# Halves of a matrix check spread among its rows, and one raw place more kept for the FFN's weights

## The chip, the core and the metric

The kernel runs on one core of one Trainium2 chip. The metric is the device time of one execution in microseconds (us). The kernel before took 197.28 us, the median of 3 runs (195.94 to 198.41).

## What is computed

All arrays are fp32, x is 2048 tokens by 576. The reference mixes by two Fourier matrices, adds the residual, picks the one token with the highest router score, and sends that token alone through a SwiGLU FFN of 4608 columns:

```python
a = einsum("bsd,ed->bse", layernorm(x), dft_hid_re); b = einsum("bsd,ed->bse", layernorm(x), dft_hid_im)
h = x + einsum("ts,bse->bte", dft_seq_re, a) - einsum("ts,bse->bte", dft_seq_im, b)
n = layernorm(h);  r = n @ w_r;  i = argmax(r)
y = (silu(n[i] @ w_gate) * (n[i] @ w_up)) @ w_down * sigmoid(r[i])
out = h + n;  out[i] += y
```

## The kernel before

The sequence matrices (`ct`) are cosines and sines, so a quarter of them, folded, is enough for the product, provided that what is left out mirrors what is used. The kernel does not take that on trust: it loads the mirrored parts too and compares them. Should a comparison fail, a general path that stands behind a branch computes everything again. So two streams run side by side: the products (PE) and the comparisons (VectorE subtracts or adds two tiles into a buffer Q of two slots, and ScalarE squares and sums a slot, `L405`, 2944 wide for a full slot).

**Two groups.** The row blocks of `ct` are worked off as group zero, `[1..5]`, and group one, `[6, 7, 0, 8]`. Each block has a cosine (0) and a sine part (1). The parts that are multiplied are kept in 14 places of D: D0 (5 places), D1 (5) and D2 (4); D0 serves group zero's cosines and later group one's sines. What is only compared goes through 8 raw places R0 to R7 (R0 to R2 are 1152 wide, R3 to R7 896), or through a D place that has come free.

**Comparisons.** A *row comparison* (`c_check`) compares one block with its mirror, which GpSimd gathers (`load_c`, 0.46 MB, 128 x 896), and, if the block has a partner (16 minus its number), the partner's block, which SyncE loads (0.59 MB, 128 x 1152), and the partner's mirror. These are the VectorE instructions of `L418` and `L420`, two of 896 and one of 1152 elements a row; `L418` is the form that also sums, used while a spill flag is open or for the last, the *gate* comparison, (8, 1). A *half comparison* (`c_half`, `off_h`) compares the two halves of blocks in D: group zero's three are on VectorE (`L449`, blocks 0 and 1, 2 and 3, and 4 of the group, cosine and sine), group one's on GpSimd (`L447`), behind the gate comparison. `w_check` and `wc_check` compare the hidden matrix W in the same way; `w_first` and `wc_first` load it.

**Products.** For each group five sequence products (`seq_step`, PE, `L641`, into PSUM tiles ps_0 to ps_4, the last 64 wide in two parts), each drained by ScalarE (a copy, `os`, `L655`) and VectorE (into Z, `L659`) in `keep_step`. PSUM has two pairs of banks for them: a product can start when Z of the last but one is out of its pair. The right-hand operand is XF, the folded and normalised x. Then the hidden products (`hid_step`, PE, `L686`, py), residual sums on VectorE (`L695`), sums of squares on ScalarE (`L718`), and router dots on VectorE (`L699`).

**The order.** The program is written as a plan: `add` names an engine, a duration in us, and what an operation needs; `Plan.order` is a list scheduler that puts the operations of all engines into the order in which they are issued, by the longest way to the end. The loads of one queue stay in the order in which the program asks for them. `ring` hands out the first free place of a list; a place is put back on that list when the program has asked for the row's comparison. So the order of the calls `c_half`, `c_check`, `w_first` decides which place each load gets, and after which comparison its engine may issue it.

**FFN weights.** They come as 1.18 MB loads (`load_ffn`, `L1330`, SyncE) into 16 spots that reuse XF, D, R, W, Z and Q. The order of loads is gate, up and down for four columns at a time. A load waits for the last reader of its spot, and everything behind it in SyncE's queue waits too. `LEFT` names raw places that, from a given row of group one on, the row comparisons do not take any more (the set `shut` in `ring`), so that the FFN weights find them free. The chosen token's products with gate and up are on VectorE (`L1347`, `L1354`) and GpSimd (`L1358`), the sums on ScalarE (`L1363`), the down product on PE (`L1384`).

Of the kernel before, what the change touches and what calls it, by code (L numbers as in the profile page):

```python
# [37 lines left out]
GROUPS = [[1, 2, 3, 4, 5], [6, 7, 0, 8]]  # L38
# [5 lines left out]
HALVES = [[(0, 2), (2, 2), (4, 1)], [(0, 2), (2, 2)]]  # L44
# [17 lines left out]
LATE = 6  # L62


LEFT = {(7, 0): (0, 1)}

# [7 lines left out]
class Plan:  # L76
# [6 lines left out]
    def add(self, eng, dur, fn, *deps, tail=0.0, push=0.0, holds=False, moves=False):  # L83
        flat = []
        for d in deps:
            flat += d if isinstance(d, list) else [d]
        n = {"eng": eng, "dur": dur, "fn": fn, "deps": [d for d in flat if d], "tail": tail, "push": push}
        n["holds"], n["moves"] = holds, moves
        n["i"] = len(self.ops)
        self.ops.append(n)  # L90
        return n
# [72 lines left out]
def kernel(  # L164
# [272 lines left out]
    def half_on_pool(g, c, i):  # L437
        return g == 1
# [343 lines left out]
    def then(f, *args):  # L782
        return lambda: f(*args)
# [41 lines left out]
    for a, b in X_RUNS:  # L825
# [4 lines left out]
        m = [add("ACT", 0.95, then(measure, k), f, push=push) for k, f in zip(ks, r)]  # L830
# [28 lines left out]
    for k in FOLDED:  # L859
        dg, use, at = [], [], []  # L860
        for sl in slots_of(k):
            n = next(places)
            UF[sl] = LATER[n]
            at.append(PLACE[n])
            if k in PAIRS:
                u, w = dgs.take()
# [42 lines left out]
    def c_load(j, i, mirror):  # L909
        CU[j, i, mirror] = ring("POOL" if mirror else "SP", load_c, 0.46 if mirror else 0.59, j, i, mirror)  # L910

    def c_first(g, i, cs=None):

        for c, j in enumerate(GROUPS[g]):
            if cs is not None and c not in cs:
                continue
            u = D_TAG[g, i], c
            if u in free:
                free.remove(u)
            w, users[u] = users[u], []  # L920
            LAST["SP"], d = load("SP", then(load_c, None, j, i, False), 0.59, w, LAST["SP"])
            CU[j, i, False] = u, d

    def c_half(g, c, m):
        u, w = qs.take()
        cus = [[CU[j, i, False] for j in GROUPS[g][c : c + m]] for i in range(2)]
        n = [
            add(
                *(("POOL", 0.3 + 1.31 * m) if half_on_pool(g, c, i) else ("DVE", 0.16 + 0.62 * m)),
                then(off_h, g, c, m, i, u), [d for _, d in cus[i]], w, PASSED if half_on_pool(g, c, i) else None,  # L930
                holds=not half_on_pool(g, c, i),
            )
            for i in range(2)
        ]
        for i in range(2):
            for b, _ in cus[i]:
                users[b].append(n[i])
        if (g, c + m) == (1, len(GROUPS[1])):
            HELD.append((u, 9 * m * P, n))
            return  # L940
        squares(u, 9 * m * P, n)
# [5 lines left out]
    def squares(u, w, n, ps=P, behind=None):  # L947
        SQUARES.append(add("ACT", 0.3 + w / 1200, then(square, u, w, ps), n, behind))
        qs.users[u].append(SQUARES[-1])

    def c_check(j, i):

        u, w = qs.take()
        u0, d0 = CU[j, i, False]
        c_load(j, i, True)
        u1, d1 = CU[j, i, True]
        n = [add("DVE", 1.08, then(off_s, j, i, u, 0), d0, d1, w, holds=True)]
        if (j, i) == GATE:
            PASSED.append(add("POOL", 0.1, lambda: pool.tensor_copy(gate[:, 1:2], gate[:, 0:1]), n))
        users[u0] += n  # L960
        users[u1] += n
        free.append(u1)
        if j in PAIRS:
            m = NK - j
            c_load(m, i, False)
            c_load(m, i, True)
            (u2, d2), (u3, d3) = CU[m, i, False], CU[m, i, True]
            n.append(add("DVE", 1.08, then(off_s, m, i, u, 1), d2, d3, w, holds=True))
            users[u3].append(n[1])
            n.append(add("DVE", 1.36, then(off_t, j, i, u), d0, d2, w, holds=True))  # L970
            users[u0].append(n[2])
            users[u2] += n[1:]
            free.extend([u3, u2])
        if u0[0] == "D1":
            free.append(u0)
        squares(u, QW if j in PAIRS else 7 * P, n)
# [3 lines left out]
    def w_first():  # L980
        for n in range(3):
            LAST["SP"], d = load(
                "SP", then(load_w, None, n), (0.59, 0.59, 0.005)[n], LAST["SP"], users["W" + "ABC"[n]]
            )
            WL.append(d)

    def wc_first():
        LAST["POOL"], d = load("POOL", then(load_w, None, 5), 0.295, LAST["POOL"])
        WC.append(d)

    def w_check():
        for n in range(2):
            u, d = ring("POOL", load_w, 0.59, n + 3)
            q, w = qs.take()
            o = add("DVE", 2.2, then(off_w, n, q), WL[n], d, w, holds=True)
            users[u].append(o)
            squares(q, 3 * D, o)
            WS.append(o)
            free.append(u)

    def wc_check():
        q, w = qs.take()
        WS.append(add("DVE", 2.6, then(off_wc, q), WL[2], WC, w))
        squares(q, D + 289, WS[-1])
# [91 lines left out]
        for b in [b for b in free if type(b) is tuple and b[0] == tag]:  # L1096
            free.remove(b)

    for c, m in HALVES[0]:
        c_half(0, c, m)  # L1100
    for n, j in enumerate(GROUPS[0]):
        if n == 3:
            w_first()
        if n == 3:
            wc_first()
        c_check(j, 0)
    for n in (0, 1, 4, 2, 3):
        seq_step(0, n)
        keep_step(0, n)
# [8 lines left out]
    no_more("D2")  # L1118
    free += [("D0", n) for n in range(N_D["D0"])]
    rows, first = iter(GROUPS[0]), iter(range(len(GROUPS[1])))  # L1120
    for step in "sffsffwcsss":
        if step == "s":
            c_check(next(rows), 1)
        elif step == "f":
            c_first(1, 0, (next(first),))
        elif step == "c":
            wc_check()
        else:
            w_check()
    no_more("D0")  # L1130
    c_first(1, 1)
    for i in range(2):
        for j in GROUPS[1]:
            shut.update(LEFT.get((j, i), ()))
            c_check(j, i)
# [103 lines left out]
    step = add("DVE", 0.25, T["steps"][0], SCORES)  # L1239
    most = add("PE", 0.4, T["steps"][1], step)  # L1240
    step = add("DVE", 0.45, T["steps"][2], step)
    step = add("PE", 0.4, T["steps"][3], step, most)
    qx = add("DVE", 0.4, from_result, SCORES)
    rows = add("DVE", 0.55, T["steps"][4], most)
    slot = add("DVE", 1.1, token, step, rows)
    step = add("DVE", 1.0, where, slot, qx)
    step = add("ACT", 2.0, row_of_token, step, slot, RESULTS)
    squares(*HELD[0], behind=step)
    near = add("POOL", 1.0, other_rows, slot, push=50.0)
    step = add("PE", 1.2, to_all, step)  # L1250
# [33 lines left out]
    for b in range(NJ // TW):  # L1284
        j = TW * b
# [202 lines left out]
    with tc.If(T["mv"], preferred_fallthrough_block=False):  # L1488
        with ExitStack() as gen:
# [33 lines left out]
            with ExitStack() as hs:  # L1523
# [9 lines left out]
                with tc.For_i(0, NK, 1) as k:  # L1533
                    dve.tensor_copy(xr, row_of(GX, k))
                    norm(xn, xr, "x")
                    for a in range(5):
                        w = min(P, D - a * P)
# [4 lines left out]
                    for c in range(4):  # L1542
                        pa = zbank(f"gpa{c}")
                        for a in range(5):
                            w = min(P, D - a * P)
# [115 lines left out]
```

## Time and profile before

| | |
|---|---|
| median of 3 runs (197.28 to compare with) | 197.28 us |
| range of the runs | 195.94 to 198.41 us |
| the profiled execution's own time | 197.32 us |
| its span on the core | 195.3 us |
| PE, weight load, VectorE, ScalarE, GpSimd busy | 67%, 46%, 84%, 72%, 61% of the span |
| moved by DMA | 77.74 MB, mean 398 GB/s |

All rows that are shown come from the one profiled execution, whose clock starts with the span; 2.0 us of its time lie around the span. Engines: PE is TensorE's matmul, DVE VectorE, ACT ScalarE, POOL GpSimd, SP SyncE; a q behind the name is the sequencer that issues DMAs. `L420` is line 420 of the kernel before; tiles have their names without numbers. In a timeline a row gives the start, the time from the first instruction's start to the last one's end, engine, line, operation, the tile written and the tiles read, their shape, and how many instructions stand in it; in square brackets how long the engine was idle before, and what ended it.

### The profile page before, as it was taken

What the parts mean: (1) busy time and instruction counts of PE and PEld (TensorE: products, weight loads), DVE (VectorE), ACT (ScalarE), POOL (GpSimd) and SP (SyncE); (2) the same over time, 40 slices, a digit from 0 to 9 for tenths busy, and PEclk for the clock granted to TensorE, in tenths of its full rate; (3) what the DMA queues carried; (4) which work ended last, traced back from release to release, by engine and by line L of the source; (5) the groups of instructions that cost most, each with busy time, mean ns of one, the idle gap of its engine ahead of it and who ended that gap; (6) DMA issues with size and microseconds to landing.
All of it is one profiled execution on the core that took longest, in us unless ns stands there. A gap on an engine that the chain in (4) does not pass through costs nothing.

```text
span 195.3 us, 2824 instructions
## 1 busy us (share of the span) xinstructions
PE 130.8 (67%) x758; PEld 89.9 (46%) x758; DVE 163.7 (84%) x430; ACT 140.4 (72%) x260; POOL 119.3 (61%) x152
## 2 busy tenths in 40 slices
PE   0007999999999999999699989800241425073960
PEld 0005667765767788677576767500121212030340
DVE  2399999999899999997799999999739999979620
ACT  3298854782898697499289979697679898986600
POOL 6588888761515874076170006968639999999500
PEclk9999999999999999999999999985555555555599
DMA  5999999999999999999999999999999999999992
GB/s 182 414 413 411 412 411 406 411 403 396 408 410 411 413 404 406 408 413 411 407 403 392 422 428 393 422 410 368 425 426 425 416 433 425 421 419 416 411 425 92
DMA packets 14483, 77.74 MB, mean 398 GB/s; under 512 B 1911, under 2 KB 1915, under 8 KB 11134
## 3 DMA queue, kind: packets, MB, share of 16 engines
q1 hardware_dynamic: 10340, 56.34, 71.5%
q0 software_dynamic: 4112, 21.17, 26.8%
q8 instruction: 7, 0.11, 0.2%
q14 instruction: 14, 0.11, 0.2%
q10 hardware_dynamic: 10, 0.00, 0.0%
HBM read 72.78 MB, written 6.49 MB: 406 GB/s over the span
## 4 chain that ended last, share of the span: by engine, by line
DVE 31%; POOL 15%; issue 15%; DMA 11%; PE 5%; ACT 2%; ACTq 0%; SPq 0%; POOLq 0%; DVEq 0%
DVE Q L420 11%; POOL D L1358 8%; DMA R<-in_ct_dram 7%; DVE junk L699 6%; DMA D<-in_wt_dram,iw 4%; DVE X L695 4%; PE pd L1384 3%; DVE Z L659 2%; POOL R L1358 2%; DVE Q L418 2%; PE pk L1392 2%; POOL R L333 1%; POOL W L1358 1%; ACT Q L405 1%; POOL Q L1358 1%
## 5 line engine op out<-in xcount | busy, mean ns | idle before, releaser
L405 ACT ACTIVATE Q<-Q 128x2944 bf16<-128x2944 bf16 (+5 forms) x26 | 54.7, 2104 | 12.7 <-DVE Q L420 7.6
L686 PE MATMUL py<-W,Z 128*128 128x289 f32 x180 | 45.3, 409 | 1.0 <-DVE X L695 1.0
L641 PE MATMUL ps<-D,XF 128*128 128x320 f32 (+3 forms) x216 | 44.9, 407 | 1.6 <-DVE Z L659 1.6
L333 POOL DMA_INDIRECT R<-in_ct_dram,ic x22 | 24.7, 1121 | 27.3 <-DVE Q L420 15.9
L686 PEld LDWEIGHTS py<-W,Z 128*128 128x128 f32 x180 | 33.7, 189 | 12.3 <-PE py L686 1.8
L641 PEld LDWEIGHTS ps<-D,XF 128*128 128x128 f32 (+1 forms) x216 | 32.2, 172 | 13.8 <-issue 3.2
L1358 POOL TENSOR_TENSOR D<-D,Z 128x1152 f32<-128x1152 f32 x7 | 18.3, 2642 | 0.0
L574 ACT ACTIVATE junk<-X,XT 128x576 bf16<-128x576 f32 x16 | 12.3, 771 | 7.5 <-DVE W L535 6.3
L718 ACT ACTIVATE junk<-X,TD 128x576 bf16<-128x576 f32 x16 | 12.3, 768 | 5.4 <-DVE X L695 5.3
L420 DVE TENSOR_TENSOR Q<-D 128x896 bf16<-128x896 f32 (+1 forms) x13 | 15.0, 1186 | 1.0 <-ACT Q L405 1.0
L418 DVE SCALAR_TENSOR_TENSOR Q<-R,D 128x896 bf16<-128x896 f32 (+1 forms) x11 | 13.4, 1216 | 2.9 <-DMA R<-in_ct_dram 2.7
L420 DVE TENSOR_TENSOR Q<-R,D 128x896 bf16<-128x896 f32 (+1 forms) x13 | 15.0, 1163 | 0.0
L613 PE MATMUL fo<-W,diag 128*128 128x288 f32 (+1 forms) x8 | 4.2, 706 | 16.0 <-DVE diag L604 16.0
L333 POOL DMA_INDIRECT D<-in_ct_dram,ic x10 | 11.9, 1189 | 4.0 <-DVE Q L420 1.8
L699 DVE SCALAR_TENSOR_TENSOR junk<-X,wrz 128x576 bf16<-128x576 f32 x16 | 12.0, 752 | 0.4
L748 ACT ACTIVATE X<-X,BB,UP 128x576 f32<-128x576 f32 x14 | 10.9, 852 | 2.0 <-DVE BB L731 2.0
L695 DVE SCALAR_TENSOR_TENSOR X<-py,X 128x576 f32<-128x576 f32 x16 | 11.7, 753 | 0.0
L1384 PE MATMUL pd<-XF,H 128*1 128x144 f32 x80 | 5.1, 406 | 9.8 <-DVE H L1376 6.1
L1363 ACT ACTIVATE junk<-D 128x576 bf16<-128x576 f32 x16 | 10.9, 683 | 0.9 <-POOL D L1358 0.3
L1384 PE MATMUL pd<-D,H 128*1 128x144 f32 x128 | 7.5, 400 | 5.4 <-DVE H L1376 5.4
L447 POOL TENSOR_TENSOR Q<-D 128x640 bf16<-128x640 f32 (+1 forms) x8 | 11.0, 1400 | 0.0
L1347 DVE SCALAR_TENSOR_TENSOR junk<-R,xsp 128x576 bf16<-128x576 f32 x14 | 10.5, 751 | 0.3
(208 smaller groups left out, 264.9 us busy)
## 6 DMA issues: line engine op xcount, KB each, us to landing
D<-in_ct_dram SPq DMA_DIRECT2D x23, 576.0 KB
R<-in_ct_dram SPq DMA_DIRECT2D x9, 576.0 KB
D<-in_wu_dram SPq DMA_DIRECT2D x4, 1152.0 KB
D<-in_wd_dram SPq DMA_DIRECT2D x4, 1152.0 KB
R<-in_wg_dram SPq DMA_DIRECT2D x3, 1152.0 KB
D<-in_wg_dram SPq DMA_DIRECT2D x3, 1152.0 KB
R<-in_wu_dram SPq DMA_DIRECT2D x3, 1152.0 KB
out_dram<-X SPq DMA_DIRECT2D x2, 1440.0 KB
```

Source lines behind the costliest of these rows:

```text
L333: pool.indirect_dma_start(tile, None, view, bass.IndirectOffsetOnAxis(ap=rows, axis=0), element_offset=at)
L405: act.activation(t, t, AF.Square, accum_out=DS[0 : t.shape[0], n : n + 1])
L418: dve.scalar_tensor_tensor(o, a, 1.0, b, op0=OP.mult, op1=op, accum_out=cell)
L420: dve.tensor_tensor(o, a, b, op=op)
L574: act.activation(junk[:, 0:D], X[:, k, 0:D], AF.Square, bias=XT[:, n : n + 1], scale=-float(D), accum_out=VX[:, n : n + 1],)
L641: pe.matmul(cm(ZP[g, n][k % 2][p0 : p0 + m], w), XF[:, q, m0 : m0 + m], DT[g, i][:, :, k, 0:HM], start=k in (0, 1), stop=k in (6, 7),)
L686: pe.matmul(YP[GROUPS[g][c]][:, h, 0:w], Z[:, a, c * P : (c + 1) * P], w_block(a)[:, h * HD : h * HD + w], start=(a == 0), stop=(a == 4),)
L695: dve.scalar_tensor_tensor(t, y, 1.0, t, op0=OP.mult, op1=OP.add, accum_out=TD[:, n, 1:2])
L699: dve.scalar_tensor_tensor(halves_of(junk2), halves_of(X[:, k, 0:D]), 1.0, YP["w"], op0=OP.mult, op1=OP.mult, accum_out=ON["dot"][:, n : n ...
L718: act.activation(junk[:, 0:D], X[:, k, 0:D], AF.Square, bias=TD[:, n, 1:2], scale=-float(D), accum_out=VAR[:, n : n + 1],)
L1358: pool.tensor_tensor(t, t, xs.unsqueeze(1).to_broadcast([P, JW, D]), op=OP.mult)
L1384: pe.matmul(T["pd"][at(h), :QD], H[:, j : j + 1], WB["d", j0][:, r, h * QD : (h + 1) * QD], start=(j == 0), stop=(j == NJ - 1),)
```

## The change

Three pieces:

- `LEFT` names the raw places 0, 1 and 3 instead of 0 and 1 from the sine row of block 7 on: place 3 is not taken any more by the last gathers.
- Group zero's cosine part was: three half comparisons, then five row comparisons with W's loads ahead of the fourth. It is now a half, two rows, a half, W's loads, three rows.
- The third half stands in the sequence behind it, after two row comparisons on sine blocks and the loads of two blocks of group one, ahead of the third row.

```diff
-LEFT = {(7, 0): (0, 1)}
+LEFT = {(7, 0): (0, 1, 3)}
...
-    for c, m in HALVES[0]:
-        c_half(0, c, m)
-    for n, j in enumerate(GROUPS[0]):
-        if n == 3:
+    pairs, rows = iter(HALVES[0]), iter(GROUPS[0])
+    for step in "hrrhwrrr":
+        if step == "h":
+            c_half(0, *next(pairs))
+        elif step == "w":
             w_first()
-        if n == 3:
             wc_first()
-        c_check(j, 0)
+        else:
+            c_check(next(rows), 0)
...
-    for step in "sffsffwcsss":
-        if step == "s":
+    for step in "sffshffwcsss":
+        if step == "h":
+            c_half(0, *next(pairs))
+        elif step == "s":
             c_check(next(rows), 1)
```

In the second string s is a row comparison, f the load of a block of group one, h a half, w and c the comparisons of W. Lines behind the second piece are three higher after the change (`L1330` is `L1333`).

The change moves instructions on all engines through the plan. SyncE's first loads, the piece of the difference with W's loads (X is the input, D and R are the places):

```order
-L394 DMA R<-in_ct_dram 128x1152 x3
+L394 DMA R<-in_ct_dram 128x1152 x2
 L465 DMA W<-in_wt_dram 128x2x576 x2
 L467 DMA W<-in_wt_dram 2x576
+L394 DMA R<-in_ct_dram 128x1152
 L394 DMA D<-in_ct_dram 128x1152
 L394 DMA R<-in_ct_dram 128x1152 x2
```

W's three loads stand one raw load earlier in the queue than before. SyncE's FFN loads, from the last load of `ct` on, before:

```order
L394 DMA R<-in_ct_dram 128x1152
L1330 DMA R<-in_wg_dram 128x2304
L1330 DMA XF<-in_wu_dram 128x2304
L1330 DMA XF<-in_wd_dram 128x2304
L1330 DMA D<-in_wg_dram 128x2304
L1330 DMA D<-in_wu_dram 128x2304
L1330 DMA D<-in_wd_dram 128x2304
L1330 DMA R<-in_wg_dram 128x2304
L1330 DMA R<-in_wu_dram 128x2304
L1330 DMA D<-in_wd_dram 128x2304
```

and after:

```order
L394 DMA R<-in_ct_dram 128x1152
L1333 DMA R<-in_wg_dram 128x2304
L1333 DMA XF<-in_wu_dram 128x2304
L1333 DMA XF<-in_wd_dram 128x2304
L1333 DMA D<-in_wg_dram 128x2304
L1333 DMA D<-in_wu_dram 128x2304
L1333 DMA R<-in_wd_dram 128x2304
L1333 DMA R<-in_wg_dram 128x2304
L1333 DMA D<-in_wu_dram 128x2304
L1333 DMA D<-in_wd_dram 128x2304
```

The sixth and the eighth load have changed between D and R. The last two gathers of mirrors go to D1.1 and D1.2 instead of R3 and R4, so it is the eighth load (into D1.1) and no longer the seventh (into R2, R3 and R4) that waits for the gate comparison. VectorE between the first and the fifth Z of group one, before (py are the hidden products, X the residual, TD its sums):

```order
L659 SCALAR_TENSOR_TENSOR Z<-ps_1_606,os_1_624 128x4x64 x2
L420 TENSOR_TENSOR Q<-D 128x896
L420 TENSOR_TENSOR Q<-R,D 128x896
L695 SCALAR_TENSOR_TENSOR X,TD<-py_3_650,X 128x576
L659 SCALAR_TENSOR_TENSOR Z<-ps_2_694,os_2_724 128x4x64 x2
L695 SCALAR_TENSOR_TENSOR X,TD<-py_3_650,X 128x576
L420 TENSOR_TENSOR Q<-R,D 128x896
L420 TENSOR_TENSOR Q<-D 128x1152 x2
L659 SCALAR_TENSOR_TENSOR Z<-ps_3_714,os_3_756 128x4x64 x2
```

and after:

```order
L420 TENSOR_TENSOR Q<-R,D 128x1152
L420 TENSOR_TENSOR Q<-R 128x896
L420 TENSOR_TENSOR Q<-D 128x896
L659 SCALAR_TENSOR_TENSOR Z<-ps_1_607,os_1_628 128x4x64 x2
L420 TENSOR_TENSOR Q<-R,D 128x896
L420 TENSOR_TENSOR Q<-D 128x1152
L695 SCALAR_TENSOR_TENSOR X,TD<-py_3_650,X 128x576 x2
L420 TENSOR_TENSOR Q<-R,D 128x896
L695 SCALAR_TENSOR_TENSOR X,TD<-py_4_672,X 128x576
L659 SCALAR_TENSOR_TENSOR Z<-ps_2_697,os_2_731 128x4x64 x2
L695 SCALAR_TENSOR_TENSOR X,TD<-py_4_672,X 128x576
L659 SCALAR_TENSOR_TENSOR Z<-ps_3_714,os_3_737 128x4x64 x2
```

Between Z of ps_1 and Z of ps_2 there were two comparisons and one residual sum; now there are three comparisons and three residual sums, and a third comparison has come ahead of Z of ps_1. The first row after the change is the comparison that waited longest for a load before (there it stood as `L418`, two rows ahead of Z of ps_1).

## The prediction

> **What bounds the kernel now.** I read the tenths of busy time first, then the chain that ended last, then windows over its stages. The page's rows for the 40 slices (each 4.88 us):
>
> ```profile
> DMA  5999999999999999999999999999999999999992
> GB/s 182 414 413 411 412 411 406 411 403 396 408 410 411 413 404 406 408 413 411 407 403 392 422 428 393 422 410 368 425 426 425 416 433 425 421 419 416 411 425 92
> ```
>
> From the second slice to the last but one the DMA engines are busy 9 tenths or more and move about 410 GB/s. So only a gap in the transfers can be won or lost there. The chain that ended last (start, length, link):
>
> ```profile
> 80.74 13.28 DMA R<-in_ct_dram
> ...
> 120.84 0.83 DVE junk L699 x2
> ...
> 137.50 1.21 PE pmt L287 x4
> ...
> 175.25 2.66 POOL D L1358
> ...
> 187.78 2.18 PE pd L1384 x64
> ```
>
> It runs from the load of a raw place issued at 80.74 us to the row comparison that waited for it, along VectorE to the scores and the choice of the token (137.50), then along GpSimd's products to the down projection. Windows of the two long stages, and the single microseconds in which the transfers thin out (duration, busy time and instructions of PE, weight load, DVE, ACT and POOL, granted clock, DMA share, GB/s):
>
> ```profile
> 94.00:137.00 43.00, 30.08 (x142) 21.88 (x141) 41.79 (x99) 34.81 (x54) 20.10 (x23) 0.92 1.01 405
> 146.80:183.40 36.60, 14.62 (x196) 6.69 (x197) 31.63 (x84) 30.91 (x86) 36.27 (x14) 0.50 1.02 423
> 98.00:99.00 1.00, 1.00 (x6) 0.88 (x5) 1.00 (x2) 1.00 (x1) 0.59 (x1) 1.00 0.89 327
> 107.00:120.00 13.00, 12.39 (x50) 9.06 (x49) 12.96 (x27) 11.73 (x20) 1.22 (x2) 1.00 1.02 425
> 120.00:121.00 1.00, 1.00 (x6) 0.76 (x5) 0.96 (x5) 0.97 (x5) 1.00 (x2) 1.00 0.81 286
> ```
>
> VectorE is busy 41.79 of 43.00 us, then GpSimd 36.27 of 36.60, and the DMA engines are full beside both. The end is therefore held by two chains at once. Of gaps, 120 to 121 costs 1 − 286/425 = 0.33 us and 98 to 99 some 0.2: about 0.5 us is all that better timed loads could win in this stretch.
>
> **The change, up to the row that waited.** Call t0 the start of that row, at 94.11 us. VectorE, the stage's head (start, busy time, idle before):
>
> ```profile
> 94.11 1.36 DVE L418 SCALAR_TENSOR_TENSOR Q<-R,D 128x1152 bf16<-128x1152 f32 x1 [2.70 <-DMA R<-in_ct_dram]
> 95.39 1.09 DVE L420 TENSOR_TENSOR Q<-R 128x896 bf16<-128x896 f32 x1
> 96.40 0.75 DVE L659 SCALAR_TENSOR_TENSOR Z<-ps,os 128x256 f32<-128x256 f32 x2
> 99.06 0.75 DVE L695 SCALAR_TENSOR_TENSOR X<-py,X 128x576 f32<-128x576 f32 x1
> 99.74 0.74 DVE L659 SCALAR_TENSOR_TENSOR Z<-ps,os 128x256 f32<-128x256 f32 x2
> 102.08 2.62 DVE L420 TENSOR_TENSOR Q<-D 128x1152 bf16<-128x1152 f32 x2
> 117.60 1.11 DVE L418 SCALAR_TENSOR_TENSOR Q<-R,D 128x896 bf16<-128x896 f32 x1
> ```
>
> Moving the halves changes which place comes free when, not how much is compared. The rows that carry this, of VectorE (the third half, the row that is the last to read the place D0.4, and the last row ahead of W's comparison), of SyncE's loads that wait for such places, and VectorE's own wait for a square:
>
> ```profile
> 41.56 1.15 DVE L449 TENSOR_TENSOR Q<-D 128x256 bf16<-128x256 f32 x3
> 58.89 1.08 DVE L420 TENSOR_TENSOR Q<-R 128x896 bf16<-128x896 f32 x1
> 66.87 1.08 DVE L420 TENSOR_TENSOR Q<-R 128x896 bf16<-128x896 f32 x1
> ```
>
> ```profile
> 50.08 3.92 SPq L394 DMA_DIRECT2D D<-in_ct_dram  x2
> 55.93 3.39 SPq L394 DMA_DIRECT2D D<-in_ct_dram  x4
> 64.34 0.33 SPq L394 DMA_DIRECT2D R<-in_ct_dram  x1
> ```
>
> ```profile
> DVE Q L420 <- ACT Q L405: 1.4, 2, 1.0
> 66.00:70.00 4.00, 4.00 (x19) 3.24 (x18) 4.00 (x8) 3.05 (x3) 3.39 (x3) 1.00 1.01 409
> ```
>
> The raw places of the first rows come free earlier, since two rows now stand ahead of a half: by the halves' lengths some 3 us. D0.4 comes free later, since its half now stands just ahead of W's comparison, at about 66 instead of 59 us. SyncE's queue is in order, so the load into D0.4 and the raw load behind it (64.34) wait there; GpSimd's own gathers fill the engines meanwhile. The bytes ahead of t0 stay the same and the engines have no gap to lose (1.01, 409), so I leave t0 where it is. Bounds: 2.70 us sooner, if the early places pull the load of 80.74 forward by all that VectorE waited; 2.9 us later, if D0.4's load and its follower (2 × 0.59 MB at 0.41 MB a us) find no cover. W's loads go one place earlier in SyncE's queue: 1.33 MB move ahead of 0.59 MB, at most 3.2 us for that raw load, which waits for a place anyway. I put 0 on all of it, nearer to the full window's row than to either bound. The two or three comparisons more that also sum (L418) cost about 0.1 us each; the 2.70 us before t0 cover those ahead of it.
>
> Why the load of 80.74 does not simply come sooner: it took 13.28 us, with gathers of GpSimd issued after it. The Trainium skill, "DMA: Bandwidth & Descriptors", section "Queues, rings and completion order", says that each DMA engine goes round robin, packet by packet, between the rings that have work. The trace agrees: 13.28 us for 0.59 MB that needs 1.4 us alone.
>
> **From t0 to the first FFN loads.** This is the term. PE's third and fifth sequence product, ACT's square and copy, SyncE's FFN loads and GpSimd's last gathers:
>
> ```profile
> 97.29 8.16 PE L641 MATMUL ps<-D,XF 128*128 128x256 f32 x54 [1.58 <-DVE Z L659]
> ```
>
> ```profile
> 101.34 0.87 PE L641 MATMUL ps<-D,XF 128*64 128x256 f32 x6
> ```
>
> ```profile
> 96.57 2.66 ACT L405 ACTIVATE Q<-Q 128x2944 bf16<-128x2944 bf16 x1 [3.94 <-DVE Q L420]
> 99.23 0.36 ACT L655 ACTIVATE os<-ps 128x256 f32<-128x256 f32 x1
> ```
>
> ```profile
> 96.51 0.33 SPq L394 DMA_DIRECT2D R<-in_ct_dram  x1
> 96.93 0.38 SPq L1330 DMA_DIRECT2D R<-in_wg_dram  x1
> 103.35 0.33 SPq L1330 DMA_DIRECT2D XF<-in_wu_dram  x1
> 118.74 0.33 SPq L1330 DMA_DIRECT2D R<-in_wg_dram  x1
> ```
>
> ```profile
> 96.75 0.94 POOL L333 DMA_INDIRECT R<-in_ct_dram,ic  x1 [4.13 <-DVE Q L420]
> ...
> 100.27 0.95 POOL L333 DMA_INDIRECT R<-in_ct_dram,ic  x1 [0.30 <-issue]
> ```
>
> The load into XF at 103.35 overwrites what the last sequence product (64 wide, from 101.34) still reads: it goes 2.0 us into it. That product needs the PSUM banks that ps_2's Z empties. Today this Z ends at 99.74 + 0.74 = 100.5, before PE is ready, and does no harm. In the new order ps_2's Z stands behind more: from t0, 1.28 + 1.01 + 1.00 (three comparisons, by the starts above), 0.7 (Z of ps_1), 1.00 + 1.28 (two comparisons), 1.35 (two L695), 1.00 and 0.68, together 9.3, so 103.4; and its copy on ACT stands behind a square that can begin when the fifth of these comparisons ends, at 100.4. From the square's start to the copy's end it is 99.23 + 0.36 − 96.57 = 3.0 us by the rows above, so the copy ends at 103.4 to 103.5. Z ends at 104.2. PE starts the last product 0.2 later, at 104.4 in place of 101.34, and the XF load goes at 106.4: 3.0 us later than now.
>
> What covers it: bytes already issued. From the thin microsecond at 98, which follows the issue at 96.51 by 1.5 us, come one raw load of 0.59 MB, one FFN load of 1.18 and three gathers of 0.46, together 3.15 MB, or 7.7 us at 0.41: they last until 105.65. An issue flows about 1.4 us later (118.74 was late, and the thin microsecond is 120 to 121). Today: 103.35 + 1.4 = 104.75, in time. The check on this count: five loads of 1.18 MB from 105.65 last 14.4 us, to 120.05, which is where the dip is. After: 106.4 + 1.4 = 107.8, so the engines run dry for 2.15 us. On the other side the dip at 120 goes: seven loads instead of six now precede the one that waits for the gate comparison, and they last until 107.8 + 17.3 = 125.1, past the gate's end at about 120.8. Back: 0.33 and a tenth around it. Net on the DMA side: +1.75 us.
>
> The page "DMA: Bandwidth & Descriptors" of the Trainium skill, section "Latency and other measured facts", gives about 0.6 us to the first byte of a load from SyncE; an estimate by it would be 0.8 us less dry time, +0.95. The rows here show 1.4 to 1.5, and the sum goes by these.
>
> **The compute chain** has the same comparisons. After ps_2's Z there is a wait of 0.1 to 0.2 us twice, for copies on ACT; the gate comparison stands two L699 (0.83 each by the chain's steps) further back and ends near 120.8 instead of 118.7, which leaves 0.4 us of true delay. I take +0.6, between 0.4 and 0.9. The later Z of the fifth product delays PE's last groups by 2.4 us, and those end behind VectorE's own work, as they do now.
>
> **The sum.** How much of the 1.75 reaches the end depends on the products:
>
> ```profile
> 180.82 2.62 POOL L1358 TENSOR_TENSOR R<-R,Z 128x1152 f32<-128x1152 f32 x1 [0.33 <-SPq L1488]
> ```
>
> GpSimd works back to back until there, and waits 0.33 us once: the loads arrive just in time, so the later of two shifts counts, +0.6 (compute) or +1.75 less up to 2 us of slack that I cannot see in rows. I take the middle, +1.2. The profiled execution lasted 197.32 us (span 195.3 and 2.0 around it), 0.04 above the median of 197.28. **Forecast: 197.3 + 1.2 = 198.5 us**, its own range 197.7 to 199.2.
>
> **Rivals.**
>
> *A. The earlier raw places pull t0 forward.* For: 2.70 us of waiting at t0, and 1.4 us for squares early on which the spread of halves can remove. Against: full engines, and no earlier byte in them. All of the later VectorE work moves up, but the end can win no more than the gaps: about −0.6, 196.7 us.
>
> *B. The place does not do what it says, or pays exactly.* LEFT only renames places from the row (7, 0) of group one on; if SyncE's queue ends its waits in the same order, the extra seventh load earns its 0.4 us and the late Z costs the same, or the list planner's costs differ from the chip's so that ps_2's Z is ready anyway (ACT's square finishing sooner). 197.3 us.
>
> *C. D0.4 holds SyncE's queue up.* Place: the load into D0.4 (SyncE, around 50 to 66 us), price 2.9 us for two loads and up to 4.3 for three: 197.3 + 2.9 to 4.3 = 200.2 to 201.6 us. It decides as soon as GpSimd's gathers (about twelve free places) do not fill the engines, that is when a slice between 58 and 68 us falls below 380 GB/s. For: SyncE's queue keeps its order, and the raw place is freed by a row. Against: the gathers on GpSimd, which have a queue of their own, get their places sooner.
>
> **How the numbers follow.** Forecast 0.45, A 0.22, B 0.18, C 0.15. The range from 196.4 to 200.6 takes in A and B and the lower part of C. A measurement of this kernel tells about 2% from no change, 3.9 us: faster than 193.3 has no case with a price, 0.02; slower than 201.2 is the upper half of C, 0.07; the rest, 0.91, is within 2%.
>
> **What would show it.** Right: the first XF load issued at t0 + 11 to 13 us instead of t0 + 9.2, one thin stretch at about 106 to 108 us with under 250 GB/s for a microsecond or two, no dip near 120, seven FFN loads issued ahead of the gate comparison's end, and ps_2's Z waiting for ACT. Wrong: the XF load still within t0 + 10 (B); t0 below 92.5 (A); t0 above 96, with a thin slice at 58 to 68 (C). If t0 stays and the XF load is late but the time is no longer than before, it is the step from dry time to the end that failed.

## The result

The changed kernel took 199.44 us, the median of 18 runs (198.51 to 200.12), beside 196.50 us for the kernel before (18 runs, 195.71 to 198.41): a ratio of 1.0146, 95% interval 1.0127 to 1.0165, or 2.9 us slower. The forecast was 198.5 with a range from 196.4 to 200.6. The way and the place were right; the size was not: +1.2 us were forecast, and 199.44 lies outside the forecast's own range (197.7 to 199.2), though inside the wide one. The forecast had also started from 197.28 us, the median of three runs of the kernel before, 0.8 us above that of the eighteen; that it came out within 0.9 us of the time, although it missed more than half of the loss, is in part luck. The profiled execution has a span of 198.0 us, 2.7 more than before's. The ratios below leave out executions over 1.5% above the fastest of their kernel (one of e2's, three of e3's, two of e7's), and e3's profile is of one of these, 200.83 us.

Busy tenths and rate of the changed kernel, slices of 4.95 us:

```profile
DMA  6999999999999999999997999999999999999992
GB/s 185 419 412 411 409 413 405 400 408 404 409 409 410 414 404 407 407 411 408 351 411 241 374 421 430 417 421 345 429 424 420 431 425 425 423 419 415 413 425 101
```

Before, no slice between the first and the stores near 135 us fell under 392 GB/s; now the 20th has 351 and the 22nd 241. The chain that ended last:

```profile
80.61 14.39 DMA R<-in_ct_dram
95.08 1.21 issue
96.29 2.09 DVE Q L420 x2
98.96 2.36 DVE Q L420 x2
101.41 2.75 ACT Q L405 x2
104.46 0.76 DVE Z L659 x2
...
138.50 1.21 PE pmt L287 x4
```

It starts with the same load, which took 14.39 us instead of 13.28, and then runs through ScalarE's square (101.41) into ps_2's Z, the step that the prediction had named. The two long stages and the thin microseconds:

```profile
94.00:137.00 43.00, 31.38 (x143) 23.76 (x141) 40.98 (x93) 34.19 (x54) 19.63 (x21) 0.93 0.97 378
146.80:183.40 36.60, 12.40 (x178) 5.69 (x178) 31.51 (x86) 29.98 (x82) 33.68 (x13) 0.50 1.01 423
98.00:99.00 1.00, 0.00 (x0) 0.00 (x0) 1.00 (x4) 1.00 (x1) 0.35 (x1) 1.00 0.74 183
100.00:103.00 3.00, 3.00 (x9) 2.37 (x8) 3.00 (x7) 1.75 (x3) 2.38 (x2) 0.50 1.04 423
106.00:107.00 1.00, 1.00 (x13) 0.79 (x10) 1.00 (x3) 0.97 (x3) 0.00 (x0) 1.00 0.82 337
107.00:108.00 1.00, 1.00 (x13) 0.79 (x11) 1.00 (x2) 1.00 (x4) 0.00 (x0) 1.00 0.13 38
108.00:109.00 1.00, 1.00 (x12) 0.83 (x10) 1.00 (x2) 0.97 (x3) 0.00 (x0) 1.00 0.82 129
109.00:110.00 1.00, 1.00 (x9) 0.51 (x5) 1.00 (x2) 1.00 (x4) 0.00 (x0) 1.00 0.78 295
120.00:122.00 2.00, 2.00 (x10) 1.56 (x9) 2.00 (x7) 1.97 (x7) 0.56 (x2) 1.00 1.04 433
```

From 106 to 110 the transfers miss (4 × 410 − 337 − 38 − 129 − 295) / 410 = 2.05 us; the dip at 120 is gone; and VectorE, 41.79 us busy before, is busy 40.98. One row was in no one's sight: from 100 to 103 PE was granted half its clock. How that comes about is in the timelines of VectorE, PE, ScalarE and SyncE's queue:

```profile
95.02 1.36 DVE L420 TENSOR_TENSOR Q<-R,D 128x1152 bf16<-128x1152 f32 x1 [4.28 <-DMA R<-in_ct_dram]
...
98.30 0.75 DVE L659 SCALAR_TENSOR_TENSOR Z<-ps,os 128x256 f32<-128x256 f32 x2
...
104.46 0.76 DVE L659 SCALAR_TENSOR_TENSOR Z<-ps,os 128x256 f32<-128x256 f32 x2
```

```profile
91.63 4.12 PE L641 MATMUL ps<-D,XF 128*128 128x256 f32 x18
99.19 5.81 PE L641 MATMUL ps<-D,XF 128*128 128x256 f32 x18 [3.44 <-DVE Z L659]
105.36 4.11 PE L641 MATMUL ps<-D,XF 128*64 128x256 f32 x36 [0.36 <-ACT Q L405]
```

```profile
101.41 2.66 ACT L405 ACTIVATE Q<-Q 128x2944 bf16<-128x2944 bf16 x1 [1.25 <-DVE Q L420]
...
104.06 0.36 ACT L655 ACTIVATE os<-ps 128x256 f32<-128x256 f32 x1
```

```profile
97.41 0.33 SPq L394 DMA_DIRECT2D R<-in_ct_dram  x1
...
107.34 0.33 SPq L1333 DMA_DIRECT2D XF<-in_wu_dram  x1
...
121.40 0.33 SPq L1333 DMA_DIRECT2D D<-in_wu_dram  x1
```

t0 is 95.02, 0.91 later. The first XF load goes at 107.34, 3.99 later than before. The 3.99 add up: 0.91 for t0; 1.0 because ps_1's Z stands at t0 + 3.28 instead of t0 + 2.29, so that PE starts ps_3 at t0 + 4.17 instead of t0 + 3.18; and 2.1 from ps_3's start to ps_4's (99.19 to 105.36, before 97.29 to 101.34). The last part has two causes at once: PE, idle 3.44 us, does ps_3's 18 matmuls in 5.81 us instead of 4.05, its clock at half from 100 to 103, and ends them at 105.0; and ps_2's Z, behind ScalarE's square, ends at 105.2. Either alone would have held ps_4 back by nearly as much. At the far end GpSimd now waits for a load, 2.07 us where it was 0.33:

```profile
183.56 2.63 POOL L1361 TENSOR_TENSOR D<-D,Z 128x1152 f32<-128x1152 f32 x1 [2.07 <-SPq L1491]
```

GpSimd's products began at 147.80, 1.0 us later than before. Of the 2.7 us of span, 1.0 is thus the compute chain's and 1.7 this wait's.

### The profile page after: what moved, and what is told of

Its sections match the earlier page's. It is cut to its first block, busy times and chain, and to the rows that moved or that the text cites. A ratio compares the mean times of both kernels' runs of the same rounds, so it can differ in the third digit from the quotient of the medians.

```text
span 198.0 us, 2819 instructions
## 1 busy us (share of the span) xinstructions
PE 132.9 (67%) x758; PEld 93.3 (47%) x758; DVE 163.7 (83%) x430; ACT 140.4 (71%) x260; POOL 121.5 (61%) x152
## 3 DMA queue, kind: packets, MB, share of 16 engines
HBM read 72.78 MB, written 6.49 MB: 400 GB/s over the span
## 4 chain that ended last, share of the span: by engine, by line
DVE 31%; DMA 21%; issue 16%; POOL 14%; PE 13%; ACT 2%; ACTq 0%; SPq 0%; POOLq 0%; DVEq 0%
DVE Q L420 9%; DMA R<-in_ct_dram 7%; POOL D L1361 6%; DVE junk L699 6%; PE fo L613 5%; DMA R<-in_ct_dram,ic 5%; DMA X<-in_x_dram,ix 4%; DMA R<-in_wt_dram,iw 4%; DVE X L695 3%; PE pd L1387 3%; PE ps L641 2%; PE pk L1395 2%; POOL R L1361 2%; POOL XF L1361 2%; ACT Q L405 1%
## 5 line engine op out<-in xcount | busy, mean ns | idle before, releaser
L641 PE MATMUL ps<-D,XF 128*128 128x320 f32 (+3 forms) x216 | 46.9, 417 | 3.8 <-DVE Z L659 3.4
L641 PEld LDWEIGHTS ps<-D,XF 128*128 128x128 f32 (+1 forms) x216 | 35.4, 178 | 15.0 <-issue 6.1
L1361 POOL TENSOR_TENSOR D<-D,Z 128x1152 f32<-128x1152 f32 x8 | 20.9, 2638 | 2.1 <-SPq L1491 2.1
L420 DVE TENSOR_TENSOR Q<-R,D 128x896 bf16<-128x896 f32 (+1 forms) x14 | 15.9, 1144 | 4.3 <-DMA R<-in_ct_dram 4.3
L333 POOL DMA_INDIRECT D<-in_ct_dram,ic x11 | 12.8, 1165 | 9.6 <-DVE Q L420 6.5
L574 ACT ACTIVATE junk<-X,XT 128x576 bf16<-128x576 f32 x16 | 12.3, 771 | 7.7 <-DVE W L535 3.3
L718 ACT ACTIVATE junk<-X,TD 128x576 bf16<-128x576 f32 x16 | 12.3, 768 | 3.0 <-DVE X L695 2.8
L420 DVE TENSOR_TENSOR Q<-D 128x896 bf16<-128x896 f32 (+1 forms) x12 | 14.0, 1195 | 0.0
L1366 ACT ACTIVATE junk<-D 128x576 bf16<-128x576 f32 x18 | 12.3, 683 | 2.1 <-POOL D L1361 1.1
L418 DVE SCALAR_TENSOR_TENSOR Q<-R,D 128x1152 bf16<-128x1152 f32 (+1 forms) x10 | 12.5, 1253 | 0.7 <-DMA R<-in_ct_dram 0.5
L1350 DVE SCALAR_TENSOR_TENSOR junk<-D,xsp 128x576 bf16<-128x576 f32 x14 | 10.5, 751 | 0.4
L613 PEld LDWEIGHTS fo<-W,diag 128*128 128x128 f32 x8 | 2.5, 331 | 17.0 <-DVE diag L604 16.1
```

What stands on the lines that cost most here:

```text
L333: pool.indirect_dma_start(tile, None, view, bass.IndirectOffsetOnAxis(ap=rows, axis=0), element_offset=at)
L418: dve.scalar_tensor_tensor(o, a, 1.0, b, op0=OP.mult, op1=op, accum_out=cell)
L420: dve.tensor_tensor(o, a, b, op=op)
L574: act.activation(junk[:, 0:D], X[:, k, 0:D], AF.Square, bias=XT[:, n : n + 1], scale=-float(D), accum_out=VX[:, n : n + 1],)
L613: pe.matmul(t[:, :w], DG[s], UF[s][:, c : c + w], start=(s == k), stop=(s != k))
L641: pe.matmul(cm(ZP[g, n][k % 2][p0 : p0 + m], w), XF[:, q, m0 : m0 + m], DT[g, i][:, :, k, 0:HM], start=k in (0, 1), stop=k in (6, 7),)
```

## The experiments

All ran beside the kernel before, 5 rounds each, and each ratio is to the kernel before with its 95% interval. In the runs e3 to e8 a short function behind the planner, `sooner`, moves an operation within the finished order of its engine: ((1, 0, 3),) stands for ps_1, its copy 0 places sooner on ScalarE, its Z 3 places sooner on VectorE. The other engines' orders, and who gets which place, stay.

What the profiles of all runs show beside each other; the missing time is (410 − GB/s) / 410 × 44 us over the window from 90 to 134 us, t0 is the start of the row that the prediction names so, and PE's idle time is the longest stretch ahead of one of its products between 90 and 128 us:

| run | t0, wait ahead | longest PE idle | first XF load | GB/s, 90 to 134 | missing us | span − 195.3 | ratio |
|---|---|---|---|---|---|---|---|
| before | 94.11, 2.70 | 1.58 | 103.35 | 410 | 0 | 0 | 1 |
| changed | 95.02, 4.28 | 3.44 | 107.34 | 385 | 2.7 | 2.7 | 1.0146 |
| e1 LEFT alone | 92.69, 0 | 2.52 | 103.06 | 400 | 1.1 | 0.9 | 1.0106 |
| e2 halves alone | 94.26, 3.24 | 2.44 | 106.15 | 394 | 1.7 | 1.5 | 1.0080 |
| e3 changed, ps_2's Z | 95.72, 4.42 | 3.44 | 108.78 | 370 | 4.3 | 3.8 | 1.0092 |
| e4 changed, ps_1's Z | 95.30, 3.75 | 5.26 | 108.91 | 370 | 4.3 | 3.9 | 1.0148 |
| e5 changed, both Zs | 95.34, 3.75 | 2.04 | 105.60 | 395 | 1.6 | 1.5 | 1.0064 |
| e6 before, both Zs | 93.96, 0.31 | 0.97 | 103.11 | 409 | 0.1 | 0.3 | 1.0031 |
| e7 before, ps_1's Z later | 92.78, 0 | 0.79 | 104.01 | 413 | −0.3 | −0.6 | 1.0016 |
| e8 as e3, ps_2 twice | 94.54, 3.60 | 0.81 | 105.59 | 401 | 1.0 | 1.2 | 1.0100 |
| e9 changed, gathers later | 91.71, 0.71 | 2.04 | 104.03 | 405 | 0.5 | −0.4 | 1.0060 |
| e10 third half alone | 93.77, 1.12 | 0.35 | 104.01 | 408 | 0.2 | 0.1 | 1.0042 |
| e11 changed, third half back | 93.32, 0 | 2.05 | 105.63 | 406 | 0.4 | 0.4 | 1.0129 |
| e12 before, gathers later | 92.54, 0 | 0.58 | 102.82 | 401 | 1.0 | 0.5 | 1.0028 |

The columns "missing" and "span" are the account of this case: in fourteen profiles they agree within 0.5 us, but for e9 (0.9). What a run's transfers lack between 90 and 134 us comes out at the end nearly in full: every run moves 77.7 MB, and from 134 to 170 us all run at 414 to 426 GB/s, so little is made up there; e9, the exception, has 426 against 417 before, which makes up 0.8 us. The ratios follow more loosely, since a profile is one execution and a kernel's runs spread by 1 to 4 us; e11 shows how far the two can part.

**e1, the raw place alone.**

```diff
-LEFT = {(7, 0): (0, 1)}
+LEFT = {(7, 0): (0, 1, 3)}
```

> Only the raw place more (LEFT), the halves as before. Theory O (the order of the Zs after the row that waits decides when the first load into XF may go, and the gap before it is the loss): the Z of ps_1 and of ps_2 stand one and two comparisons further back than before, so the first XF load should go at about t0 + 10.5 us instead of t0 + 9.2, with a gap of about half of the full change's, no dip near 120 us, and a time 0.5 to 1.2 us above before. Theory Q (the halves' places hold SyncE's queue up and make the row's load late): t0 stays within 0.3 us of 94.1 and the time is that of before, within 0.4 us.

Ratio 1.0106 (1.0058 to 1.0155), 2.1 us. Slower, as theory O had it, but by more than its 0.5 to 1.2 us, and not at the place it named: the XF load goes at 103.06 and there is no gap there. The loss lies at 126 to 130 us:

```profile
118.00:122.00 4.00, 4.00 (x11) 2.88 (x10) 3.82 (x11) 3.90 (x9) 1.89 (x3) 0.57 1.01 424
126.00:130.00 4.00, 3.30 (x14) 2.24 (x12) 3.12 (x7) 3.35 (x6) 4.00 (x4) 1.00 0.88 320
```

PE was idle 2.52 us for a residual sum (its bank) before 117.6, then had half its clock, and the load into W, which waits for PE's last hidden products, went at 128.39 instead of 125.36. The seven loads ahead of the gate comparison did come, without a gain. Up to the row (7, 0), where LEFT begins to act (by its key this is part 0 of block 7, not the sine part as the section on the change has it), the program asks for the same places as before, yet t0 is 92.69, and e7, whose edit too acts only behind t0, has 92.78: from one profile to the next t0 moves by 1.4 us by itself. The profile, of one of the two shortest executions, shows 0.9 us of the 2.1.

**e2, the halves alone.** The diff of the change without the line on LEFT.

> Only the halves spread, LEFT as before. Theory O: Z of ps_1 and ps_2 at about t0 + 3.3 and t0 + 7.5 us, XF load at about t0 + 10.5, a gap of about 1 us before it, the dip near 120 us still there, time 1.0 to 2.0 us above before. Theory Q: t0 about 0.9 us later than before, as in the full change, and the whole loss of 2.9 us here.

Ratio 1.0080 (1.0047 to 1.0113). Theory O's order of size, and more than the order: t0 + 11.9 for the XF load, since PE, idle 2.44 us, has 0.57 of its clock from 98 to 102:

```profile
98.44 9.81 PE L641 MATMUL ps<-D,XF 128*128 128x256 f32 x54 [2.44 <-DVE Z L659]
```

```profile
98.00:102.00 4.00, 3.56 (x9) 2.94 (x10) 4.00 (x9) 3.41 (x8) 3.17 (x5) 0.57 1.00 394
```

The dip near 120, expected to stay, is gone (415 GB/s from 120 to 122). Theory Q's whole loss is not there, and t0, 94.26, is not 0.9 later. The two pieces alone add up to 1.9%, the two together cost 1.5%, within the intervals.

**e3 and e4, one Z sooner.**

```diff
-    todo = plan_ffn(best[1])[1]
+    todo = sooner(plan_ffn(best[1])[1], KEEP, ((2, 1, 4),))
```

```diff
-    todo = plan_ffn(best[1])[1]
+    todo = sooner(plan_ffn(best[1])[1], KEEP, ((1, 0, 3),))
```

> The changed kernel with ps_2's copy and Z moved ahead (the copy by one square on ScalarE, the Z by two residual sums, one comparison and one residual sum on VectorE), nothing else. Theory O as predicted (ps_2's Z alone sets the last sequence product): the XF load goes at about t0 + 9.2 instead of t0 + 12.3, the gap of 2 us closes, time 1.5 to 2.0 us below the changed kernel. Rival P (PE was idle 3.44 us before ps_3, its clock then stood at 0.50 for 3.5 us, and ps_3 ended only at 105.0 us): the last product starts with ps_3's end, the XF load gains 0.4 us at most, time within 0.4 us of the changed kernel.

> The changed kernel with ps_1's Z moved ahead of the row that waits for its load, into VectorE's 4.3 us of waiting, nothing else. Rival P: PE goes from ps_2 to ps_3 without an idle stretch, its clock stays at 1.00, ps_3 ends near t0 + 5 us; ps_2's Z, now 0.7 us sooner on VectorE but still behind the square on ScalarE, then sets the XF load at about t0 + 11.7 to 12; time 0.5 to 1.0 us below the changed kernel. Theory O as predicted: ps_3's start does not matter, time 0 to 0.7 us below, by VectorE's 0.7 us alone.

e3: ratio 1.0092 (1.0054 to 1.0130), of nine executions. The median of all twelve, 199.09 us, is 1.4% above before's, so no gain on the changed kernel is shown. One of the twelve took 308.38 us, without a trace, so that its cause is open. The XF load did not move to t0 + 9.2: it went at t0 + 13.1. Theory O in the form of the prediction, that ps_2's Z alone sets it, is refuted here. Rival P has the reason, PE's clock, but not its size: the clock was at 0.50 from 99 to 105 us, twice as long as in the changed kernel. e4: ratio 1.0148 (1.0098 to 1.0198), no gain at all. The idle stretch only moved. PE in e3 and in e4, and the clock behind the idle stretch of each:

```profile
99.89 8.39 PE L641 MATMUL ps<-D,XF 128*128 128x256 f32 x30 [3.44 <-DVE Z L659]
```

```profile
105.20 6.49 PE L641 MATMUL ps<-D,XF 128*64 128x256 f32 x36 [5.26 <-ACT Q L405]
```

```profile
100.00:104.00 4.00, 4.00 (x10) 3.19 (x11) 4.00 (x9) 3.03 (x4) 2.97 (x3) 0.50 0.99 403
```

```profile
104.00:110.00 6.00, 4.80 (x24) 3.06 (x26) 5.89 (x12) 5.28 (x13) 0.49 (x1) 0.50 0.62 217
```

With ps_1's Z early, PE waits 5.26 us for ps_2's, the last product takes 6.49 us instead of 4.1, and the gap is longer than in the changed kernel. VectorE's 0.7 us, won in the wait, went with it.

**e5, both Zs sooner.** `((1, 0, 3), (2, 1, 4))`.

> The changed kernel with both Zs sooner: ps_1's into VectorE's wait for the row's load, ps_2's (and its copy) ahead of the residual sums. Theory C (PE idle of 2.4 us or more before a sequence product puts its clock at 0.50 for about 3.5 us; an earlier ps_1 or ps_2 alone only moves the idle stretch): PE is never idle over 1.6 us between 92 and 106, the clock stays at 1.00, the XF load goes at t0 + 8 to 9 us, the gap of 2 us before it is gone, and the time is 1.5 to 2.5 us below the changed kernel, 197 to 198 us where before is 196.4. Theory T (the time is lost through the later row and the order of the comparisons as such): 198.5 us or more, as with either Z alone.

Ratio 1.0064 (1.0034 to 1.0094): 0.8%, or 1.6 us, under the changed kernel. Neither Z alone gains, both together do, as theory C expected of the time and of the gap: from 105 to 110 us 370 GB/s move, against 234 in the changed kernel. Its picture of PE is not met: the XF load is at t0 + 10.3 instead of t0 + 8 to 9, as PE still idles 2.04 us before ps_4 and has 0.57 of its clock from 102 to 106. Of the 1.6 us that are still missing, 1.1 are from 97 to 100 us (264 GB/s), where SyncE's next load waits for the late row.

```profile
102.01 5.79 PE L641 MATMUL ps<-D,XF 128*64 128x256 f32 x36 [2.04 <-DVE Z L659]
```

```profile
102.00:106.00 4.00, 3.99 (x22) 2.90 (x24) 3.91 (x11) 3.73 (x6) 2.49 (x4) 0.57 1.01 401
```

**e6 and e7, the same moves in the kernel before.** `((1, 0, 2), (2, 1, 3))` and, the other way, `((1, 0, -2),)`.

> The kernel before with ps_1's Z moved into the wait for the row's load, and ps_2's copy and Z one square and three VectorE places sooner. Theory C: the 1.58 us of PE idle before ps_3 go, XF load near t0 + 7 to 8 us instead of t0 + 9.2, the thin microsecond at 106 goes, VectorE has 0.7 us less behind the row; the dip near 120 stays. Time 0.3 to 0.8 us below before. Rival: the transfers are full anyway, time within 0.2 us of before.

> The kernel before with ps_1's Z moved two comparisons back, nothing else: PE is then idle about 3.5 us before ps_3 instead of 1.6. Theory C: the clock falls to 0.50 for about 3.5 us, ps_3 takes 5.8 us instead of 4.1, the XF load goes at about t0 + 12.5 us, a gap of about 2 us before it, time 1.5 to 2.5 us above before. Rival without the clock: ps_3 from about 99.2 to 103.3, XF load at t0 + 11, gap 0.7 us, time 0.3 to 0.8 us above before.

e6: ratio 1.0031 (1.0007 to 1.0056), no gain: PE's idle stretch and the thin stretch at 106 went, but the XF load stayed at t0 + 9.2 instead of t0 + 7 to 8, since PE came to ps_2 1.6 us later and had no pause up to ps_4's end, and the dip at 120 to 122 grew (281 GB/s instead of 355). e7: 1.0016 (0.9989 to 1.0042), a miss: in its profile the row's load had landed before VectorE was there, PE's idle time fell to 0.79 us, and so the run says nothing on the clock. It does say that two comparisons ahead of ps_1's Z are harmless where t0 is early. Two of its twelve executions took 199.44 and 199.81 us; whether the row was late in them is open, as they left no trace.

**e8, PE kept busy.** e3 with the sequence product of ps_2 done twice into the same banks:

```diff
-        for q, k in enumerate(FOLDED):
+        for q, k in [*enumerate(FOLDED)] * (2 if (g, n) == (1, 2) else 1):
```

> As the run with ps_2's Z alone sooner, but PE multiplies ps_2 twice (the same product into the same banks, 4 us more of PE work that does not change the result), so PE is busy while it waits for ps_1's Z. Theory C: the clock stays at 1.00, ps_3 and ps_4 run in 4.1 us each, the XF load goes at t0 + 10 to 10.5 us although PE has done more, against t0 + 13.1 in that run; time 0.5 to 1.5 us below it. Rival (the idle time as such, not the clock): the added 4 us of matmuls bring nothing, XF load and time as in that run or later.

```profile
91.83 15.85 PE L641 MATMUL ps<-D,XF 128*128 128x256 f32 x90
```

```profile
96.00:106.00 10.00, 10.00 (x58) 8.03 (x58) 9.91 (x20) 7.93 (x10) 5.25 (x5) 1.00 1.01 380
```

With 4 us more of work PE is done sooner: no idle stretch, clock 1.00, XF load at t0 + 11.05 against t0 + 13.06. So it is the clock, and not the wait as such, that put the load at t0 + 13.06 in e3's profile. The time, 1.0100 (1.0053 to 1.0147), cannot be told from e3's.

**e9, the gathers ahead of t0 later.** In `load_c` of the changed kernel:

```diff
         if mirror:
+            mirrors.append(j)
+            if len(mirrors) == 25:
+                for _ in range(18):
+                    pool.memset(rest, 0.0)
```

> The changed kernel with 18 small memsets on GpSimd behind the first of the seven gathers that are issued just ahead of t0, so that the other six go about 1.5 us later, as they do in the kernels with the halves in their old place. In ten profiles so far t0 was 92.7 to 94.1 us where those gathers began at 83.0 to 84.6 and 94.3 to 95.7 where they began at 82.2 to 82.7. Theory G (gathers issued sooner take more of the shared engines ahead of the row's load and make it land later): t0 comes 0.7 to 1.5 us sooner, 93.5 to 94.3, and the time falls by 0.4 to 1.2 us below the changed kernel. Rival: the gathers' start does not matter, t0 stays at 94.5 to 95.5 and the time within 0.3 us of the changed kernel.

Ratio 1.0060 (1.0032 to 1.0089): 0.9%, or 1.7 us, under the changed kernel, by 18 instructions that do nothing. GpSimd and VectorE (lines of this kernel are 4 higher):

```profile
82.42 1.68 POOL L333 DMA_INDIRECT R<-in_ct_dram,ic  x1 [8.62 <-DVE Q L422]
84.10 2.78 POOL L392 MEMSET rest<- 128x2 f32 x18
87.54 1.47 POOL L333 DMA_INDIRECT R<-in_ct_dram,ic  x1 [0.66 <-DVE Q L424]
```

```profile
91.71 1.36 DVE L424 TENSOR_TENSOR Q<-R,D 128x1152 bf16<-128x1152 f32 x1 [0.71 <-DMA R<-in_ct_dram]
```

Five gathers go 3.0 to 4.5 us later than in the changed kernel (the second at 84.14 there), more than the 1.5 that were meant, and the row's load, issued at 80.87, is in by 91.71 instead of 95.02. Theory G holds in this profile: 91.71 is outside all that t0 was without the memsets. With t0 at 91.7 PE goes from ps_2 to ps_3 without a pause, and the gap before the XF load is closed: it is still at t0 + 12.3, but at 104.0. PE idles 2.04 us before ps_4, as in e5, and here its clock stays:

```profile
102.05 4.11 PE L645 MATMUL ps<-D,XF 128*64 128x256 f32 x36 [2.04 <-ACT Q L409]
```

```profile
102.00:106.00 4.00, 3.95 (x36) 2.98 (x36) 4.00 (x7) 3.94 (x10) 0.00 (x0) 1.00 1.03 404
```

**e10 and e11, the third half.** e10: the kernel before with the third half in its new place only. e11: the changed kernel with the strings "hrrhwrhrr" and "sffsffwcsss".

> The kernel before with the third half alone moved to its new place ahead of W's comparison; the first two halves stand first and W's loads where they were, LEFT as before. If the third half causes the later row (its place D0.4 holds SyncE's queue, GpSimd's gathers fill in): t0 at 94.3 us or later with over 3 us of waiting on VectorE, PE idle 2.4 us or more before ps_3, its clock at 0.5, time 1.0 to 2.0 us above before, as with all halves spread. If the first two cause it: t0 92.7 to 94.1, time within 0.6 us of before.

> The changed kernel with the third half in the first string (half, two rows, half, W, row, half, two rows) and LEFT as changed. If the third half causes the later row: t0 at most 94.1 us, time 0.8 to 2.0 us below the changed kernel. If the first two halves (or W's place) cause it: t0 94.3 or later, time within 0.6 us of the changed kernel.

e10: t0 93.77, PE never idle over 0.35 us from there to the end of the hidden products, ratio 1.0042 (1.0018 to 1.0066), which lies between the two cases expected: the third half alone is a quarter to a third of the loss, and does not make the row late. e11: t0 93.32 without a wait; XF load at t0 + 12.3, since the order behind t0 is the changed one; ratio 1.0129 (1.0087 to 1.0171), not to be told from the changed kernel. Neither of the two cases expected came: the row is early and the time is long. The profile is of one of its two short executions (197.49 us; four of six took 198.41 to 199.55), and it lacks another 0.8 us of transfers at 82 to 84 us (248 GB/s), outside the table's window; what made the four long is open. In the six profiles of kernels with all halves spread and the gathers as they come, t0 is 94.26 to 95.72; in the six others without the memsets, e10 and e11 among them, it is 92.69 to 94.11. Neither piece of the spread moves it there alone; with one profile each and a scatter of 1.4 us, which of them does it stays open.

**e12, the gathers later in the kernel before.** The edit of e9.

> The kernel before with the same 18 memsets on GpSimd (2.8 us) behind the first of the seven gathers ahead of t0, nothing else. Theory G (later gathers let the row's load through): t0 at 91 to 92.5 us instead of 94.1, VectorE's 2.7 us of waiting gone, the XF load at t0 + 9.2, 100.5 to 102; since the transfers are full the end gains little, 0 to 0.8 us below before. Rival (the gathers' data are then late for the rows behind t0, or the gain at t0 was the changed kernel's alone): t0 at 93.5 or later or new waits on VectorE behind it, time at or above before.

Ratio 1.0028 (0.9999 to 1.0057). VectorE's wait is gone (the row runs at 92.54). That is no test of theory G, since e1 and e7 ran without the wait, at 92.69 and 92.78, with the gathers as they come. The wait's absence is worth nothing here, and the row of the transfers says why.

```profile
92.00:100.00 8.00, 8.00 (x39) 6.93 (x38) 8.00 (x15) 6.06 (x8) 6.16 (x8) 1.00 1.00 354
```

Before moved 401 GB/s there, and e1 and e7 moved 410 and 407. The late gathers leave the engines with fewer bytes; what the wait gave was paid in bytes. No version beat the kernel before.

## Why the prediction came out as it did

- *The transfers hold the end, and a gap in them is what can be lost*: right, and more strictly so than I used it. The table shows it.
- *t0 stays*: wrong by 0.91 us in the profile. I had argued that the bytes ahead are the same. They are: when the row's load is issued, SyncE's queue has moved 18.59 MB before and 18.54 after, the gathers 13.25 and 13.24. But the load shares the engines with gathers that are issued after it, and these moved 2.79 MB up to t0 instead of 2.49; in e9, with five of them held back, 1.51 MB, and t0 is 3.3 us sooner. The rule on round robin that the prediction cites from the Trainium skill, "DMA: Bandwidth & Descriptors", section "Queues, rings and completion order", was the one to follow to its end: it bears on what comes after the load as well, and e9's trace agrees. Why the gathers got more in the changed kernel is open. That they were issued sooner (from 82.16 instead of 82.97) does not settle it: in e10 all six stand within 0.1 us at the same distances behind the load, yet they moved 1.61 MB, and the load was in after 11.1 us instead of 14.4.
- *ps_2's Z ends at t0 + 10.1, the XF load goes at t0 + 12.3*: 104.46 + 0.76 = t0 + 10.2, and 107.34 = t0 + 12.3. Right to 0.1 us. That it was the only cause was not so: the prediction has no term for PE's clock, and PE, for 3 us at half clock, ended ps_3 within 0.3 us of the same moment, which is why e3 gained nothing there.
- *Dry for 2.15 us, the dip at 120 back*: 2.05 us, and gone. But t0's 0.9 us also widened the gap at 97 to 100 (335, 183 and 364 GB/s: 0.85 us missing, before some 0.3).
- *Compute chain +0.6*: +1.0, of which 0.9 is t0.
- *The middle between +0.6 and +1.75*: this is the step that failed. There was no slack: GpSimd's wait for loads grew from 0.33 to 2.07 us, and the whole of the lost transfer time, 2.7 us, came out at the end. With the full 1.75 the forecast would have been 199.1, and with the 0.55 us by which t0 widened the first gap 199.6; the profiled execution took 199.79.
- *Rival A* (sooner raw places, t0 forward): gathers did go sooner, but the row came later, not sooner. *Rival B*: the place did what it says (seven loads ahead of 121.40), and the dip of 0.33 us went; e1 shows no gain by the place alone. *Rival C*: SyncE's queue did stand still for D0.4 (11.2 us behind the third half), and the gathers covered it, 409 to 414 GB/s in the 12th to 14th slice. Its mechanism was there without its price.

## What to carry to other kernels

Where transfers are full nearly throughout, price a reordering by the bytes that are not moved while queues run empty, and let all of it reach the end unless a row shows slack. An instruction that drains PSUM for the next product sets two things, when the next operand's memory comes free and whether PE keeps its clock: here either drain moved alone gained nothing, and both together did. A wait that ends on a load is not yet a cost: e1, e7 and e12 ran without it and none was faster than before; e9, where its end also closed a gap, gained on the changed kernel.

## What the runs showed of the hardware

From 30 to 128 us PE's clock fell to half after idle stretches of 2.44 us (0.57 over the next 4 us, e2), 2.52 (0.57, e1), 3.44 (0.50 from 100 to 103), 5.26 (0.50, e4), and after 2.04 in e5 but not after 2.04 in e9 or 2.05 in e11; never after 1.73 (e7, before 83.3) or less. By the traces' records of the granted clock the half lasted 3.41 us in the changed kernel, e1, e2 and e5, and 6.83 us in e3 and e4: the same 3.44 us of idling cost one such stretch in the changed kernel and two in e3. The Trainium skill, "TensorE: Matmul & The Clock Gate", section "What's actually happening", has a free-running window of about 3.4 us, and half clock after a window of idling. The traces agree with a window that runs free (2.04 us gives both outcomes) and with half-clock stretches of one or two such windows; that the idle stretch must fill a whole window they do not bear out.

Gathers of 0.46 MB, issued by GpSimd behind a load of SyncE's, bear on when that load lands: by 91.7 us with five of them held back 3.0 to 4.5 us, at 95.0 without, for a load issued at 80.9 and 80.6. Between issue and landing SyncE's queue moved 2.9 to 3.1 MB in both, in the kernel before and in e10, the gathers 1.5 (e9), 1.6 (e10), 2.5 (before) and 2.8 MB (changed); the load took 10.8, 11.1, 13.3 and 14.4 us.
